# A gated linear-attention kernel: gates with two steps per partition, un-permuted in 64-row matmuls, with sine and cosine from two PSUM banks

## The chip, the cores and the metric

The kernel runs on one core of one Trainium2 chip. The metric is the device time of that core in microseconds (us), as a median over several executions. Engines are named as in the profile: PE is TensorE, PEld its weight loads, DVE is VectorE, ACT is ScalarE, POOL is GpSimd, SP issues DMAs. The profile also shows PEclk, the share of its full clock that TensorE was granted.

A run is called slow when its time is over 1.5% above the fastest run of the same kernel.

## The reference, cut to what matters

Two parts follow each other. The first is a linear attention with a complex decay, for 4 batches, 8 heads, 768 steps and a head width of 48. The second is a layer norm with a two-layer MLP of widths 384, 1536 and 384.

```python
mag = np.sqrt(a_re*a_re + a_im*a_im)
scale = np.minimum(mag, 0.999) / (mag + 1e-06)
a_re_n, a_im_n = a_re*scale, a_im*scale
for t in range(S):
    new_re = ar*S_re - ai*S_im          # ar, ai: step t of a_re_n, a_im_n, per row of the state
    new_im = ar*S_im + ai*S_re
    S_re, S_im = new_re + k[t] (x) v[t], new_im
    y[t] = q[t] @ S_re
# x = y with the heads side by side: (4, 768, 384)
xn = (x - mean) / sqrt(var + 1e-06) * g_ln
out = x + relu(xn @ w_ch1) @ w_ch2
```

Over a chunk of 128 steps, the product of the decays is the exponential of a running sum of logarithms (`l`), and its angle is a running sum of angles (`th`). So the kernel computes running sums by triangular matmuls, takes `exp`, `sin` and `cos`, multiplies them into q and k, and then works with plain matmuls per chunk: scores `at`, output `y`, state `G`. There are 24 chunks.

## The kernel before

The gates are made for a group of three chunks at a time. A step of the sequence is a partition. The calls are put in order by a plan with real-number positions, and each engine runs its own list in that order.

The gates and the running sum of the logarithms:

```python
def g_decay(g, cs):                       # DVE
    nc.vector.scalar_tensor_tensor(out=cut(l, cs), in0=cut(G[g]["u"], cs), scalar=0.5,
                                   in1=cut(G[g]["w"], cs), op0=ALU.mult, op1=ALU.add)
    nc.vector.tensor_scalar(out=cut(l, cs), in0=cut(l, cs), scalar1=LNCAP,
                            scalar2=LNEPS, op0=ALU.min, op1=ALU.add)

def s_decay(g, c):                        # one 128-row matmul, two exponentials
    nc.tensor.matmul(ps, lhsT=u_f, rhs=row(G[g]["l"], c), start=True, stop=True)
    special(out=row(e, c), in_=ps, func=AF.Exp)
    special(out=row(en, c), in_=ps, func=AF.Exp, scale=-1.0)
```

The phase: PE adds the angles and the phase carried in from the last chunk (`car`). DVE adds a constant that puts the fraction of a turn in the low 16 bits. POOL reads the last row back as the next carry. Sine comes from ACT, and cosine from DVE by a half-angle formula:

```python
def s_phase(g, c, eng=nc.gpsimd):
    nc.tensor.matmul(ps, lhsT=u_th, rhs=row(G[g]["th"], c), start=True, stop=first)
    if not first:
        nc.tensor.matmul(ps, lhsT=last[96:C, :], rhs=X[n - 1]["car"][96:C, :],
                         start=False, stop=True)
    nc.vector.tensor_scalar(out=row(ph, c), in0=ps, scalar1=WINDOW, scalar2=None, op0=ALU.add)
    if n % NCH < NCH - 1:
        eng.tensor_scalar(out=X[n]["car"][96:C, :], in0=turns(row(ph, c)[96:C]),
                          scalar1=1.0 / TURN, scalar2=None, op0=ALU.mult)

def s_cos(g, cs):
    nc.vector.tensor_tensor(out=cut(hq, cs), in0=cut(hs, cs), in1=cut(hs, cs), op=ALU.mult)
    nc.vector.tensor_scalar(out=cut(cos, cs), in0=cut(hq, cs), scalar1=-2.0, scalar2=1.0,
                            op0=ALU.mult, op1=ALU.add)
```

The MLP weights are scaled by `g_ln` once, on DVE, and centred into a second copy. The first MLP layer has one PSUM buffer `hps`:

```python
def scale(dc):
    nc.vector.tensor_scalar(out=W["w1b"][:, dc], in0=W["w1b"][:, dc],
                            scalar1=W["gln"][:, ds(dc, 1)], scalar2=None, op0=ALU.mult)

def mm1(jp):
    ps = ph.tile([C, 2, 512], FP32, tag="h", name="hps")     # pool ph: bufs=1
    ...                                                       # cut: six matmuls into ps
    nc.scalar.activation(out=st["h"][:, ts(jp, 2)], in_=ps[:, :, 0:GC * C], func=AF.Relu)
```

## Time and profile before

The time was 280.08 us, the median of three runs (278.67 to 282.95; the last is just over 1.5% above the first and so counts as slow).

The first view is the page: busy times with the share of the span and the instruction count, then the span in 40 slices of 7 us (a digit is the busy share in tenths; PEclk is the granted clock in tenths), then the chain of work that ended last, by engine ("issue" is time in which an engine waited for nothing that the profile shows).

```profile
PE 207.4 (74%) x1915; PEld 136.4 (49%) x1917; DVE 197.2 (71%) x328; ACT 175.4 (63%) x247; POOL 99.3 (36%) x107
...
PE   0321542747849996989799969988998999998673
DVE  0679906999699669986997699689848946633001
PEclk9999999999786998999799979997999999999999
...
PE 33%; DVE 32%; ACT 12%; issue 11%; POOL 8%; DMA 2%; POOLq 0%; DVEq 0%; ACTq 0%
```

No engine is full over the whole span, and the chain of waits divides itself equally between PE and DVE. The slices show why an average misleads here: DVE is at 9 in places from slice 4 on and fades at the end, while PE reaches 9 only in slice 13 (84 us).

The second view is the window view of the same trace. Its columns are the stretch in us, its length, the busy time (and instruction count) of PE, PEld, DVE, ACT and POOL, then PEclk, the DMA share and GB/s.

```profile
0.00:60.00 60.00, 21.26 (x132) 12.91 (x132) 39.03 (x61) 37.49 (x53) 26.18 (x42) 1.00 1.31 176
60.00:100.00 40.00, 30.51 (x274) 19.96 (x277) 34.63 (x62) 24.48 (x35) 18.00 (x16) 0.87 1.23 184
100.00:245.00 145.00, 132.12 (x1363) 90.60 (x1362) 117.23 (x194) 104.67 (x147) 55.08 (x50) 0.95 0.34 66
245.00:279.00 34.00, 23.47 (x151) 12.91 (x148) 6.36 (x14) 8.76 (x14) 0.00 (x0) 1.00 0.10 35
```

Before 60 us PE has little to do. In the long middle PE is busy for 132 of 145 us and DVE for 117.

The third view is the groups of instructions, by form: line, engine, operation, tiles, shape and count, then busy us and mean ns, then idle us before it.

```profile
L230 DVE SCALAR_TENSOR_TENSOR l<-u,w 128x1152 f16<-128x1152 f16 x7 | 27.2, 3886 | 3.0 <-ACT u L196 3.0
...
L281 POOL TENSOR_SCALAR car<-ph 32x384 f16<-32x384 int16 x17 | 22.1, 1300 | 79.6 <-DVE ph L277 78.5 <-ACT en L196 0.8
...
L159 DVE TENSOR_SCALAR w1b<-w1b,gln 128x1536 bf16<-128x1536 bf16 x3 | 1.9, 617 | 0.0
```

The step `l` takes 3.89 us for 1152 elements, though with POOL not in its way it takes 0.5 to 0.55 us for 384 (three such calls at the start).

Two timelines of the same moment, DVE and then POOL, show why `l` is slow. The columns are start, duration, and the instruction.

```profile
130.36 4.08 DVE L230 SCALAR_TENSOR_TENSOR l<-u,w 128x1152 f16<-128x1152 f16 x1 [0.39 <-ACT u L196]
```

```profile
130.58 2.64 POOL L301 TENSOR_TENSOR qe<-q,e 128x384 bf16<-128x384 f32 x3
```

While POOL works through its three products, `l` makes no progress to speak of: `l` ends 1.2 us after the last product, and 4.08 us less 2.64 us is 1.44 us, near its free time. The Trainium skill ("SBUF — State Buffer", section "Who interferes with whom") says that DVE and GpSimd share a port pair under an exclusive lock. This trace agrees.

One timeline of PE shows a phase before the change: one full-height matmul, one 32-row carry, and then the next work.

```profile
90.02 0.33 PE L273 MATMUL tps<-th,u_th 128*128 128x384 f16 x1
90.27 0.33 PE L275 MATMUL tps<-car,last 32*128 32x384 f16 x1
90.54 0.50 PE L416 MATMUL o<-w2b,h 128*128 128x384 bf16 x2
```

The durations overlap (0.33 us at starts 0.25 us apart), so starts are what to read: from 90.02 to 90.54 is 0.52 us for a phase. The starts after a change of row height are 0.25 to 0.27 us apart, while equal 384-column matmuls follow each other every 0.162 us (six in 1.14 us, the last one ending about 0.33 us after its start).

The last timeline is the tail, PE and ACT together.

```profile
258.85 1.14 PE L407 MATMUL hps<-xT,w1c 128*128 128x384 bf16 x6 [0.90 <-ACT h L410]
...
260.02 0.81 ACT L410 ACTIVATE h<-hps 128x768 bf16<-128x768 f32 x1 [1.22 <-PE hps L407]
...
260.88 1.14 PE L407 MATMUL hps<-xT,w1c 128*128 128x384 bf16 x6 [0.57 <-ACT h L410]
```

With one `hps` buffer the matmuls and their eviction (ACT's copy out of PSUM) take turns.

### The profile page before, as it was taken

The numbers are of one execution on the slowest core, as the hardware profiler recorded it, in microseconds if no ns is written. First come the engines' busy times: TensorE is split into PE (matmuls) and PEld (weight loads), VectorE is DVE, ScalarE is ACT, GpSimd is POOL, SyncE is SP. The second block draws the span as 40 slices with busy tenths as digits, with TensorE's granted clock in tenths as the row PEclk, the third lists the DMA queues.
The fourth block names the chain that finished last, engine by engine and source line by source line (L and its number), as shares of the span: only waits on it lengthen the run. The fifth ranks groups of instructions, "written<-read, shape, count | busy, mean of one in ns | idle before, by whom it ended". The sixth has DMA issues, their size and how long they took to land.

```text
span 279.1 us, 4840 instructions
## 1 busy us (share of the span) xinstructions
PE 207.4 (74%) x1915; PEld 136.4 (49%) x1917; DVE 197.2 (71%) x328; ACT 175.4 (63%) x247; POOL 99.3 (36%) x107
## 2 busy tenths in 40 slices
PE   0321542747849996989799969988998999998673
PEld 0000221734536664757475737564656667764331
DVE  0679906999699669986997699689848946633001
ACT  6682483754695588688777858884679663541420
POOL 4069106703870275057706530763148100000000
PEclk9999999999786998999799979997999999999999
DMA  7999999999999966473790370000000101001001
GB/s 155 214 219 184 136 196 184 142 161 190 217 194 160 159 150 134 94 151 73 152 138 2 73 153 31 2 28 31 28 2 28 60 0 59 28 2 56 28 31 56
DMA packets 130310, 28.62 MB, mean 103 GB/s; under 512 B 125296, under 2 KB 129904, under 8 KB 130288
## 3 DMA queue, kind: packets, MB, share of 16 engines
q1 hardware_dynamic: 103696, 23.60, 43.6%
q0 software_dynamic: 26592, 4.72, 20.5%
q8 instruction: 15, 0.25, 0.3%
q14 instruction: 7, 0.06, 0.1%
HBM read 28.31 MB, written 4.72 MB: 118 GB/s over the span
## 4 chain that ended last, share of the span: by engine, by line
PE 33%; DVE 32%; ACT 12%; issue 11%; POOL 8%; DMA 2%; POOLq 0%; DVEq 0%; ACTq 0%
PE o L416 14%; PE hps L407 10%; DVE l L230 7%; POOL car L281 6%; ACT h L410 4%; DVE atm L334 3%; DVE ot L421 3%; DVE ks L307 2%; DVE l L232 2%; DVE stats L371 2%; DVE qs L307 2%; ACT u L196 2%; DVE ph L277 2%; DVE hq L295 1%; PE tot L254 1%
## 5 line engine op out<-in xcount | busy, mean ns | idle before, releaser
L410 ACT ACTIVATE h<-hps 128x768 bf16<-128x768 f32 x48 | 38.8, 809 | 49.4 <-PE hps L407 49.1
L416 PE MATMUL o<-w2b,h 128*128 128x384 bf16 x288 | 62.6, 353 | 5.7 <-DVE ot L421 4.6
L407 PE MATMUL hps<-xT,w1c 128*128 128x384 bf16 x288 | 55.9, 330 | 4.7 <-ACT h L410 3.8
L281 POOL TENSOR_SCALAR car<-ph 32x384 f16<-32x384 int16 x17 | 22.1, 1300 | 79.6 <-DVE ph L277 78.5
L416 PEld LDWEIGHTS <-h 128*128 128x128 bf16 x288 | 28.6, 104 | 25.7 <-issue 11.8
L407 PEld LDWEIGHTS <-w1c 128*128 128x128 bf16 x288 | 27.8, 99 | 23.6 <-issue 9.6
L334 DVE TENSOR_TENSOR atm<-at,mask 128x512 bf16<-128x512 f32 x48 | 32.5, 679 | 3.7 <-PE at L332 3.7
L421 DVE SCALAR_TENSOR_TENSOR ot<-o,rstd,x 128x384 f32<-128x384 f32 x24 | 14.7, 611 | 26.2 <-PE o L416 25.8
L230 DVE SCALAR_TENSOR_TENSOR l<-u,w 128x1152 f16<-128x1152 f16 (+1 forms) x10 | 28.8, 2886 | 3.0 <-ACT u L196 3.0
L322 ACT COPY qsT<-tp 96x1024 bf16<-96x1024 bf16 x24 | 24.1, 1004 | 7.8 <-PE tp L320 7.8
L192 ACT ACT_TABLE_LOAD x19 | 24.4, 1283 | 1.1 <-PEq L526 0.7
L332 PE MATMUL at<-qsT,ksT 96*128 96x128 bf16 x192 | 21.0, 230 | 3.2 <-DVE G L353 2.3
L220 DVE TENSOR_TENSOR r<-aim,rinv 128x1152 f16<-128x1152 f32 (+1 forms) x10 | 11.1, 1111 | 16.9 <-DMA aim<-in_a_im_dram 10.1
L301 POOL TENSOR_TENSOR ke<-k,en 128x384 bf16<-128x384 f32 x24 | 21.6, 908 | 0.8
L307 POOL TENSOR_TENSOR qs<-qe,sin 128x1152 bf16<-128x1152 bf16 x7 | 16.9, 2418 | 11.9 <-ACT sin L196 11.9
L301 POOL TENSOR_TENSOR qe<-q,e 128x384 bf16<-128x384 f32 x24 | 21.2, 903 | 0.0
L320 PE MATMUL tp<-ident,ks 128*96 128x128 bf16 x192 | 18.6, 244 | 2.6 <-DVE ks L307 1.7
L332 PEld LDWEIGHTS <-ksT 96*128 96x128 bf16 x192 | 15.2, 104 | 10.4 <-issue 7.9
L320 PEld LDWEIGHTS <-ks 128*96 128x96 bf16 x192 | 16.1, 142 | 8.2 <-issue 4.7
L322 DVE COPY ksT<-tp 96x1024 bf16<-96x1024 bf16 x24 | 16.3, 681 | 4.4 <-PE tp L320 4.3
L320 PE MATMUL tp<-ident,qs 128*96 128x128 bf16 x192 | 18.7, 238 | 0.2 <-ACT x L369 0.2
L320 PEld LDWEIGHTS <-qs 128*96 128x96 bf16 x192 | 16.1, 137 | 5.6 <-issue 3.5
(88 smaller groups left out, 379.1 us busy)
## 6 DMA issues: line engine op xcount, KB each, us to landing
are<-in_a_re_dram SPq DMA_DIRECT2D x24, 192.0 KB, 3.8
aim<-in_a_im_dram SPq DMA_DIRECT2D x24, 192.0 KB, 3.8
k<-in_k_dram SPq DMA_DIRECT2D x24, 192.0 KB, 3.8
q<-in_q_dram SPq DMA_DIRECT2D x24, 192.0 KB, 3.9
out_dram<-ot SPq DMA_DIRECT2D x24, 192.0 KB, 1.9
v<-in_v_dram POOLq DMA_DIRECT2D x4, 576.0 KB, 15.5
w1b<-in_moe_w_ch_dram POOLq DMA_DIRECT2D x1, 1152.0 KB, 19.0
w2b<-in_moe_w_ch_dram POOLq DMA_DIRECT2D x1, 1152.0 KB, 26.3
```

The source lines that it names most:

```text
L192: chain(nc.scalar.preload_act_table_set({"log": "natural_log_exp_and_others", "trig": "trig_and_small"}[name]))
L230: nc.vector.scalar_tensor_tensor(out=cut(l, cs), in0=cut(G[g]["u"], cs), scalar=0.5, in1=cut(G[g]["w"], cs), op0=ALU.mult, op1=ALU.add)
L281: eng.tensor_scalar(out=X[n]["car"][96:C, :], in0=turns(row(ph, c)[96:C]), scalar1=1.0 / TURN, scalar2=None, op0=ALU.mult)
L301: nc.gpsimd.tensor_tensor(out=row(t, c), in0=row(G[g][which], c), in1=row(G[g]["en" if which == "k" else "e"], c), op=ALU.mult)
L307: eng.tensor_tensor(out=t[:, cs, :, a].rearrange("p c h d -> p (c h) d"), in0=heads(G[g][which + "e"]), in1=heads(G[g]["sin" if a else "co ...
L320: nc.tensor.transpose(ps[:, h], st[which][:, c, h].rearrange("p a d -> p (a d)"), ident)
L322: (nc.scalar.copy if which == "qs" else nc.vector.tensor_copy)(out=t, in_=ps)
L332: nc.tensor.matmul(ps[:, i], lhsT=x["ks"][:, h], rhs=x["qs"][:, h], start=True, stop=True)
L334: nc.vector.tensor_tensor(out=x["atm"][:, ds(half * (H // 2), H // 2)], in0=ps, in1=mask.unsqueeze(1).to_broadcast([C, H // 2, C]), op=ALU ...
L407: nc.tensor.matmul(ps[:, ji, 0:GC * C], lhsT=W["w1c"][:, dc, ts(j, C)], rhs=st["xT"][:, dc].rearrange("p c t -> p (c t)"), start=(dc == 0) ...
L410: nc.scalar.activation(out=st["h"][:, ts(jp, 2)], in_=ps[:, :, 0:GC * C], func=AF.Relu)
L416: nc.tensor.matmul(st["o"], lhsT=st["h"][:, j, ts(c, C)], rhs=W["w2b"][:, j], start=(j == 0), stop=(j == NJ - 1))
```

## The change

The intent is to take work off DVE, POOL and ACT, and to give some of it to PE. (In the code below, "stacks" are the products of the scaled q or k with sine and cosine, `lps` holds the running sums of logarithms, `tot` their totals per chunk, `tps` the phases, and `dps` the totals laid out for the state.) A group is now four chunks. A partition holds two consecutive steps, so `a_re` and `a_im` arrive in runs of 384 bytes. Chunks come out of this layout in the matmuls: the steps of one chunk lie in 64 partitions, so each running sum is made of two 64-row matmuls. Cosine is the sine of the phase plus a quarter turn: the phase is computed twice, into two PSUM banks, and one ACT call takes both. The carry comes in by a 128-row matmul with a selecting matrix `pick`, whose right-hand side also holds the constants. DVE takes the next carry from PSUM.

The core of the diff, cut (`...`) and joined to one line here and there:

```diff
-    GC = 3
+    R = 2                        # steps per partition
+    QC = 4                       # chunks per group
-    pa = ... bufs=5              # PSUM banks
-    ph = ... bufs=1              # two banks, hps
-    po = ... bufs=1              # o
+    pa = ... bufs=4
+    pb = ... bufs=2              # two banks each: lps, tps, at, hps in turn
...
 # weights
-            nc.vector.tensor_scalar(out=W["w1b"][:, dc], in0=W["w1b"][:, dc],
-                                    scalar1=W["gln"][:, ds(dc, 1)], ...)
+        nc.gpsimd.tensor_scalar(out=w1b[:, dc], in0=w1b[:, dc], scalar1=gln[:, ds(dc, 1)], ...)
...
 # running sum of logarithms, two chunks at a time
-        nc.tensor.matmul(ps, lhsT=u_f, rhs=row(G[g]["l"], c), start=True, stop=True)
+        for j in range(R):
+            for i in range(R):
+                nc.tensor.matmul(heads(ps[:, i]), lhsT=u_f[ts(i, HALF), j],
+                                 rhs=steps(Q[qi]["l"], k_, i, j), start=(j == 0),
+                                 stop=(j == R - 1))
...
 # phase of one chunk
-        nc.tensor.matmul(ps, lhsT=u_th, rhs=row(G[g]["th"], c), ...)
-        nc.tensor.matmul(ps, lhsT=last[96:C, :], rhs=X[n - 1]["car"][96:C, :], ...)
-        nc.vector.tensor_scalar(out=row(ph, c), in0=ps, scalar1=WINDOW, ...)
-        eng.tensor_scalar(out=X[n]["car"][96:C, :], in0=turns(row(ph, c)[96:C]), ...)
+        for s in range(2):                        # sine bank, cosine bank
+            for j in range(R):
+                nc.tensor.matmul(heads(ps[:, s]), lhsT=u_th[ts(i, HALF), j],
+                                 rhs=steps(Q[qi]["th"], k_, i, j), start=(j == 0), stop=False)
+            nc.tensor.matmul(ps[:, s, 0:DM], lhsT=pick[rows, s], rhs=cars[n % 2][rows],
+                             start=False, stop=True)
+        nc.vector.tensor_scalar(out=cars[(n + 1) % 2][96:C], in0=v16[96:C, 0],
+                                scalar1=1.0 / TURN, ...)
+        special(out=trig[:, m], in_=v16, func=AF.Sin, scale=TWO_PI_SAFE / TURN)
-    s_cos: hq = hs * hs; cos = 1 - 2 hq           # DVE, both gone
...
 # stacks: one of four was on POOL, now all on DVE; scores evicted in one piece of 1024
 # plan: new table of positions (PLACES), new order of the start
```

## The prediction

> **What bounds the kernel now.** No engine is saturated: the page gives PE 74%, DVE 71%, ACT 63%, POOL 36% of 279.1 us. By stretches of the window view: 0-45 us is startup (first transposes at 32.6 us; DVE then waits 7.8 us for `aim`, behind crowded DMA); 45-165 us has DVE busy 103 of 120 us and PE 96; 165-254 us is PE (82 of 89 us); from 254 us there is a tail of 25 us, of which 12 us is `hps` matmuls and the `h` eviction taking turns (1.15 + 0.82 us, one buffer). The chain of waits says the same: PE 33%, DVE 32%, ACT 12%, issue 11%, POOL 8% (almost all `car`).
>
> **Removed.** DVE: `ph` 13.2 us, `hq` 6.3, `cos` 3.9, `w1b` scaling 1.9. POOL: `car` 22.1 and one `qs` stack 16.9 (about 39 of 99 us). ACT: about 4.5 us of exponentials (two chunks per instruction), 2 of `h`, 3 of gates, about five table loads of 1.28 us. DVE `atm` in one piece saves about 3.5.
>
> **Port sharing.** `l` takes 3.9 us for 1152 elements while `qe` runs on POOL and 0.55 us for 384 without; so 41 us of the two `l` steps should be near 14 unblocked. The Trainium skill ("SBUF - State Buffer", Who interferes with whom) says that a DVE instruction with two SBUF inputs blocks against a GpSimd instruction that reads SBUF; this trace agrees: `l` ends as the last `qe` ends. `ke`/`qe` stay on POOL, so I count on half of these 27 us only.
>
> **Added.** DVE: `car` read from PSUM, about 20 x 0.5 = 10 us, and stacks +6 us (48 of about 0.54). PE: a phase is six 384-column matmuls per chunk in place of two, a decay sum four per two chunks instead of two: 124 more matmuls. Warm spacing is 0.162 us (six `hps` in 1.14 us), so about 20 us, plus about 0.09 us at each change between 64 and 128 rows (the 32-row `car` matmul shows such a gap: next start 0.25-0.27 us later). The skill ("TensorEngine Tiling (Array Packing)", Key Properties) says that changing the mode drains the array. Together about 25 us of PE occupancy, estimated.
>
> **Sum.** From spacings I estimate real PE occupancy of 177 us now, about 200 after; DVE falls from 197 to about 175-185; ACT about 170; POOL about 60-65. So PE becomes the limit in the middle, but it has slack there. Gains on the critical path: startup works on two chunks first and `a` arrives in 384-byte pieces, so first transposes at about 20 us (-10); the wait on `aim` (-5); no POOL step in the phase chain, less blocking of DVE in the middle (-12); two `hps` buffers in the tail (-5 net, though the last group has four chunks). Against: PE work in the middle (+8).
>
> **Prediction: 257 us**, 8 in 10 between 240 and 275. Faster by over 2%: 0.84; within 2%: 0.10; slower by over 2%: 0.06.
>
> **What would show it.** First transposes near 20 us; POOL busy near 65 us; DVE below 190 us, `l` at 1.8-3 us per 1536 elements; PE busy above 225 us; tail after the last `xT` under 20 us with `hps` back to back; PE as the largest part of the chain.
>
> **What would make it wrong.** The two double-bank PSUM buffers now carry decay sums, phases, score blocks and `hps` in turn: if ACT is late with a sine, PE stalls in order, and the serial phase chain (PE, DVE `car`, PE) shows up as waits of PE. If mode changes cost more than 0.1 us, PE adds over 40 us and the gain vanishes. If the stacks, now all on DVE, collide with `ke`/`qe`, DVE gets no shorter.

## More of the kernel before

From 60 to 100 us DVE is the busiest engine (34.6 of 40).

The weight scaling is a small item: three times 0.62 us.

## The result, and the profile after

The change gave 270.19 us, the median of four runs (269.37 to 270.54), beside 280.93 us for the kernel before in the same rounds. The ratio is 0.964, with a 95% interval of 0.957 to 0.971. A ratio here and below is the mean time of a kernel's fast runs over that of the other's fast runs of the same rounds, so it is not quite the ratio of the quoted medians.

So the kernel became faster by 3.6%. The forecast was 257 us, which is 8.2%. So less than half of the expected gain came.

The page after, the same parts as before and the POOL slices as well (a slice is 6.7 us now):

```profile
PE 212.0 (79%) x1953; PEld 124.1 (46%) x1953; DVE 173.9 (65%) x277; ACT 171.8 (64%) x199; POOL 80.2 (30%) x93
...
PE   0146733389302999999999999999999999999994
...
DVE  1334238658999789985799656987578466645011
...
POOL 8390009442996770009400091000910000000000
PEclk9999999999955699999999999999999999999999
...
PE 60%; ACT 19%; DVE 15%; POOL 3%; issue 2%; POOLq 0%; DVEq 0%; ACTq 0%
```

Two things stand out. From slice 14 on, PE is at 9 in all slices but the last. Before that, in slices 11 to 13 (67 to 87 us), PE falls to 3, 0 and 2, and its granted clock to 5, 5 and 6 right after. In these slices POOL is at 9, 9 and 6.

The window view after:

```profile
0.00:60.00 60.00, 25.48 (x170) 11.76 (x170) 26.78 (x37) 30.97 (x35) 26.20 (x47) 1.00 1.05 189
60.00:100.00 40.00, 23.42 (x214) 12.20 (x213) 35.35 (x41) 26.57 (x29) 29.32 (x18) 0.79 1.28 173
100.00:245.00 145.00, 143.55 (x1463) 89.60 (x1463) 106.84 (x191) 107.12 (x130) 24.66 (x28) 1.00 0.33 62
245.00:268.00 23.00, 19.59 (x111) 10.49 (x109) 4.92 (x10) 7.12 (x9) 0.00 (x0) 1.00 0.16 61
```

In the middle PE is busy for 143.6 of 145 us: it has become a stream without gaps. From 60 to 100 us PE did less than before (23.4 us and 214 instructions, against 30.5 and 274), and POOL did more (29.3 against 18.0).

To see what each stage gained, follow one milestone: the moment at which ACT evicts the attention output `x` of a chunk. Here is the fourth one, first from the timeline of ACT before, then after.

```profile
85.05 0.48 ACT L369 CAST x<-y 128x384 bf16<-128x384 f32 x1 [0.31 <-PE y L366]
```

```profile
96.38 0.48 ACT L496 CAST x<-y 128x384 bf16<-128x384 f32 x1 [0.80 <-PE y L493]
```

| stretch | before, us | after, us | difference |
|---|---|---|---|
| start to the 4th output | 85.1 | 96.4 | +11.3 |
| 4th to the last output (20 chunks) | 166.2 | 148.6 | -17.6 |
| last output to the end | 27.9 | 23.4 | -4.5 |
| span | 279.1 | 268.4 | -10.7 |

The first output comes at 55.6 us, where it was at 54.5. The second comes at 59.6 us (before, 65.4), and only then does the new kernel fall behind: the third comes at 78.9 us (before, 76.0). The border between the first two rows is not sharp: at its fourth output the new kernel has evicted the decays of 12 chunks, the old one those of 9. In the MLP it is not ahead: its first MLP eviction starts at 105.3 us, before at 87.7 us. So the 11.3 us are no exact measure of a loss; the experiments measure that.

Three timelines of the hole after the change, DVE, POOL and PE:

```profile
71.96 3.34 DVE L334 TENSOR_TENSOR r_616<-r 128x1536 f16<-128x1536 f16 x1
...
76.95 4.19 DVE L346 SCALAR_TENSOR_TENSOR l<-r_616,w 128x1536 f16<-128x1536 f16 x1
81.17 4.40 DVE L348 TENSOR_SCALAR l<-l 128x1536 f16<-128x1536 f16 x1
```

```profile
69.69 5.67 POOL L278 TENSOR_SCALAR w1b<-w1b,gln 128x1536 bf16<-128x1536 bf16 x1
...
76.25 8.91 POOL L278 TENSOR_SCALAR w1b<-w1b,gln 128x1536 bf16<-128x1536 bf16 x2
```

```profile
70.41 0.61 PE L452 MATMUL at<-qsT,ksT 96*128 96x128 bf16 x8
85.63 1.44 PE L381 MATMUL tot<-l,sel 128*4 128x384 f16 x4 [14.61 <-DVE l L348]
```

The weight scaling, moved to POOL, runs from 69.7 to 75.4 us and from 76.3 to 85.2 us. The DVE steps end about when POOL's end: the square at 75.3 us, the second `l` at 85.6 us. The next matmul of PE's list needs `l`, so PE stands still from 71 to 85.6 us. The groups view after gives the size of the moved step:

```profile
L278 POOL TENSOR_SCALAR w1b<-w1b,gln 128x1536 bf16<-128x1536 bf16 x3 | 14.6, 4863 | 0.0
```

It is 14.6 us where it was 1.9 us.

The waits of PE after the change (what it waited for, us in total, times, longest):

```profile
PE lps L368 <- DVE l L348: 20.7, 3, 11.2
PE tot L381 <- DVE l L348: 14.6, 1, 14.6
```

Both lines are waits for `l`: of the running sums (`lps`) and of the totals (`tot`). The three of the first line end at 11.2, 35.0 and 51.5 us, in the start.

PE's timeline for one phase after, answering to the three lines of before (the matmuls marked `tp` are other work put between):

```profile
126.35 0.50 PE L406 MATMUL tps<-th,u_th 64*128 64x384 f16 x2
...
127.14 0.33 PE L409 MATMUL tps<-car_124,pick 128*128 128x384 f16 x1
127.40 0.50 PE L406 MATMUL tps<-th,u_th 64*128 64x384 f16 x2
127.83 0.34 PE L409 MATMUL tps<-car_124,pick 128*128 128x384 f16 x1
```

From 127.14 to 127.83 us is 0.69 us for one bank of three matmuls, so a chunk's phase takes 1.38 us of PE, against 0.52 us. Of that, each change between 64 and 128 rows costs about 0.1 us (a start gap of 0.26 or 0.27 us, instead of 0.162 us).

The tail after, from PE's timeline:

```profile
248.86 7.93 PE L524 MATMUL hps<-xT,w1b 128*128 128x512 bf16 x36
256.63 7.96 PE L534 MATMUL o<-w2b,h 128*128 128x384 bf16 x48
```

Two `hps` buffers removed the turns: 36 matmuls back to back, then 48.

### The profile page after: what moved, and what is told of

Same layout as the page of the kernel before. It is cut to its first block, busy times and chain, and to the rows that moved or that the text cites. A ratio compares the mean times of both kernels' runs of the same rounds, so it can differ in the third digit from the quotient of the medians.

```text
span 268.4 us, 4759 instructions
## 1 busy us (share of the span) xinstructions
PE 212.0 (79%) x1953; PEld 124.1 (46%) x1953; DVE 173.9 (65%) x277; ACT 171.8 (64%) x199; POOL 80.2 (30%) x93
## 2 busy tenths in 40 slices
DMA packets 105350, 28.62 MB, mean 107 GB/s; under 512 B 100336, under 2 KB 104944, under 8 KB 105328
## 4 chain that ended last, share of the span: by engine, by line
PE 60%; ACT 19%; DVE 15%; POOL 3%; issue 2%; POOLq 0%; DVEq 0%; ACTq 0%
PE o L534 16%; PE hps L524 11%; PE tps L406 8%; PE tp L440 6%; PE tps L409 5%; PE at L452 3%; DVE l L346 3%; PE lps L368 2%; ACT h L527 2%; ACT are L309 2%; ACT L305 2%; ACT w L309 2%; DVE r L332 2%; DVE l L348 2%; PE gm L474 2%
## 5 line engine op out<-in xcount | busy, mean ns | idle before, releaser
L524 PE MATMUL hps<-xT,w1b 128*128 128x512 bf16 x216 | 51.7, 378 | 0.2 <-ACT h L527 0.2
L534 PE MATMUL o<-w2b,h 128*128 128x384 bf16 x288 | 50.8, 326 | 0.0
L527 ACT ACTIVATE h<-hps 128x1024 bf16<-128x1024 f32 x36 | 36.5, 1021 | 11.6 <-PE hps L524 11.4
L309 ACT ACTIVATE trig<-tps 128x768 bf16<-128x768 int16 x24 | 19.5, 811 | 26.9 <-DVE car_124 L413 16.9
L534 PEld LDWEIGHTS <-h 128*128 128x128 bf16 x288 | 27.1, 98 | 17.6 <-issue 1.6
L454 DVE TENSOR_TENSOR atm<-at,mask 128x1024 bf16<-128x1024 f32 x24 | 29.2, 1217 | 7.5 <-PE at L452 7.3
L406 PE MATMUL tps<-th,u_th 64*128 64x384 f16 x96 | 26.3, 357 | 8.2 <-ACT th L309 8.2
L524 PEld LDWEIGHTS <-w1b 128*128 128x128 bf16 x216 | 19.6, 98 | 18.9 <-issue 0.5
L368 PE MATMUL lps<-l,u_f 64*128 64x384 f16 x48 | 7.7, 420 | 20.7 <-DVE l L348 20.7
L496 ACT CAST x<-y 128x384 bf16<-128x384 f32 x24 | 11.3, 472 | 13.5 <-PE y L493 13.5
L332 DVE TENSOR_TENSOR r<-aim,are 128x1536 f16<-128x1536 f32 (+1 forms) x7 | 11.7, 1665 | 11.8 <-ACT are L309 11.8
L381 PE MATMUL tot<-l,sel 128*4 128x384 f16 x24 | 6.9, 417 | 14.6 <-DVE l L348 14.6
L498 DVE BATCH_NORM_STATS2 stats<-x 128x6 f32<-128x384 bf16 x24 | 13.3, 554 | 6.8 <-ACT x L496 6.7
## 6 DMA issues: line engine op xcount, KB each, us to landing
w1b<-in_moe_w_ch_dram POOLq DMA_DIRECT2D x1, 1152.0 KB, 11.3
```

Of the source, the lines that this page charges most:

```text
L309: chain(nc.scalar.activation(**kw))
L332: nc.vector.tensor_tensor(out=cut(r, bs), in0=cut(Q[qi]["aim"], bs), in1=cut(Q[qi]["are"], bs), op=ALU.mult)
L406: nc.tensor.matmul(heads(ps[:, s]), lhsT=u_th[ts(i, HALF), j], rhs=steps(Q[qi]["th"], k_, i, j), start=(j == 0), stop=False)
L454: nc.vector.tensor_tensor(out=x["atm"], in0=ps, in1=mask.unsqueeze(1).to_broadcast([C, H, C]), op=ALU.mult)
L524: nc.tensor.matmul(ps[:, ji], lhsT=w1b[:, dc, ts(jp * 2 + ji, C)], rhs=Q[qi]["xT"][:, dc].rearrange("p c t -> p (c t)"), start=(dc == 0), ...
L527: nc.scalar.activation(out=h[jp], in_=ps, func=AF.Relu)
```

## The experiments

Two theories came from the traces. The first says that the moved weight scaling is the lost gain: it takes POOL eight times as long, it holds the port that DVE needs, and PE starves behind DVE and then runs at half clock. The second, its rival, says that PE's added work is the lost gain: PE has no gap in the middle, so each added microsecond is paid in full. Two more came up later: that ACT's table loads between the logarithm and sine sets make the early hole, and (called theory L) that the order of the first logarithms sets the start. Eighteen kernels were run; all gave the right result unless it is said.

A gain over the change that is given below in us is the difference of the two ratios to before, times the time of the change. The intervals of the ratios make such a difference uncertain by 2 to 3 us. The milestones of the section before help where this is too coarse: each is read from one trace.

### 1. The weight scaling back on DVE, at the same place

```diff
-        nc.gpsimd.tensor_scalar(out=w1b[:, dc], in0=w1b[:, dc], ...
+        nc.vector.tensor_scalar(out=w1b[:, dc], in0=w1b[:, dc], ...
```

> The changed kernel with the three weight scalings (1536 elements each) back on DVE; the order on PE, ACT and SP is the same. Theory S (starved start): on POOL they took 14.6 us, blocked the decay steps of DVE, and PE stood still from 71 to 85.6 us; since PE is a gap-free stream afterwards, what is lost early is never won back. Then the gap is gone and the time falls by 8 to 14 us, to 256 to 262 us. Rival R (PE has enough other waits early, so the gap only moves): 266 us or more.

It took 269.91 us (267.12 to 271.25), ratio 0.956 (0.950 to 0.963), not clear of the change. Theory S's figure was missed; the rival's held. Its profiled run was a slow one (clock 0.918), so only the order of events is read from it. The timeline of DVE says what happened:

```profile
57.34 3.15 DVE L278 TENSOR_SCALAR w1b<-w1b,gln 128x1536 bf16<-128x1536 bf16 x3 [5.73 <-DMA w1b<-in_moe_w_ch_dram]
```

In DVE's list the scaling now stands ahead of the scores of the first chunks, and the weights have not landed yet. DVE waited 5.73 us for them, and PE behind it. The hole moved rather than closed. This run does not test the first theory; runs 5 and 6 do.

### 2. The two carries of a phase after its four 64-row matmuls

```diff
         for s in range(2):
             for j in range(R):
                 nc.tensor.matmul(heads(ps[:, s]), lhsT=u_th[ts(i, HALF), j], ...)
+        for s in range(2):
             nc.tensor.matmul(ps[:, s, 0:DM], lhsT=pick[rows, s], ...)
```

> The changed kernel with each chunk's four 64-row phase matmuls first and its two 128-row carry matmuls after them: two changes of rows per chunk in place of four; same matmuls. Theory P (PE is the limit after 85 us and each change of rows costs about 0.1 us): a phase takes about 1.18 us of PE instead of 1.38, 16 chunks lie after 85 us, so 3 to 4 us less, 266 to 267 us. Rival (PE's stream has slack, or the changes of rows cost nothing): 269.5 us or more.

It took 266.87 us (265.90 to 268.51), ratio 0.950 (0.945 to 0.954), as expected. A phase now has two changes of row height and not four. From the start of its four 64-row matmuls to the start of the next chunk's is 1.19 us in PE's timeline, with the two carries in between, against 1.38 us:

```profile
124.14 0.82 PE L405 MATMUL tps<-th,u_th 64*128 64x384 f16 x4
...
125.33 0.82 PE L405 MATMUL tps<-th,u_th 64*128 64x384 f16 x4
```

That is 0.19 us times 24 chunks, or 4.6 us, and the time fell by 1.5% (0.9639 to 0.9495), about 4 us. This fits what the start gaps say of the changes of row height, with an uncertainty of over 2 us. By the milestones, 1.0 us came before the fourth output and 2.1 us between it and the last. The Trainium skill ("TensorEngine Tiling (Array Packing)", section "Key Properties") says that a change of tiling mode drains the engine; the run agrees, and gives the size.

### 3. No cosine bank (wrong result)

```diff
-        for s in range(2):                 # the matmuls of a phase
+        for s in range(1):
...
-        special(out=trig[:, m], in_=v16, ...)
+        special(out=trig[:, m], in_=v16[bank 0].to_broadcast([C, 2, DM]), ...)
```

> The changed kernel with the cosine bank's three matmuls of each phase left out and both planes of sines read from the first bank: a wrong result on purpose. Theory P: 0.69 us of PE per chunk goes, 16 chunks lie after 85 us, so about 11 us less, 257 to 261 us. Rival (the added matmuls hide in PE's waits): 267 us or more.

It took 262.24 us (261.70 to 263.14), ratio 0.933 (0.930 to 0.936). The relative error is 0.60, as intended. Leaving out three matmuls per chunk takes 24 x 0.69 = 16.6 us of PE away, and the time fell by 3.2%, about 8.8 us. So about half of that work was on the path to the end. Not all of it can be: in the first 90 us PE waits for others. The fourth output comes only 0.5 us earlier than in the change (95.8 us), and the stretch from it to the last falls from 148.6 to 141.3 us.

### 4. The kernel before, with the weight scaling on POOL

```diff
-            nc.vector.tensor_scalar(out=W["w1b"][:, dc], ...
+            nc.gpsimd.tensor_scalar(out=W["w1b"][:, dc], ...
```

> The kernel before, with only its three weight scalings moved from DVE to POOL. Theory S says that this move alone costs time when it meets DVE's decay steps: 4 to 12 us more than before. Rival R: within 2 us of before, or less, since DVE is relieved by 1.9 us.

It took 285.09 us (284.37 to 286.98), ratio 1.015 (1.010 to 1.020). This one line makes the old kernel about 4 us slower. (The interval is clear of 1.) Its groups view shows the same slow step: three instructions on POOL, 14.6 us together, 4.88 us each.

### 5. No weight scaling at all (wrong result)

```diff
-        nc.gpsimd.tensor_scalar(out=w1b[:, dc], in0=w1b[:, dc], scalar1=gln[:, ds(dc, 1)],
-                                scalar2=None, op0=ALU.mult)
```

> The changed kernel with the three weight scalings left out (a wrong result on purpose); the order on every engine is otherwise the same. Putting them on DVE only moved the hole in PE's stream, because DVE then waited 5.7 us for the weights to land. Theory S: without them on POOL, r, l and their followers on DVE lose about 9 us of blocked time between 68.9 and 85.6 us, the hole closes by that much, and nothing later gives it back: 260 to 264 us. Rival T (the hole is set by ACT, which loads its tables four times there): 267 us or more.

It took 263.55 us (262.64 to 263.77), ratio 0.939 (0.934 to 0.943), with a relative error of 0.47. The order of all other instructions is unchanged. That is 2.6% less than the change, about 7 us. DVE's timeline, at the place of the hole:

```profile
72.13 0.95 DVE L334 TENSOR_TENSOR r<-r 128x1536 f16<-128x1536 f16 x1
...
76.82 1.76 DVE L346 SCALAR_TENSOR_TENSOR l<-r,w 128x1536 f16<-128x1536 f16 x1 [2.15 <-ACT r L309]
78.61 0.56 DVE L348 TENSOR_SCALAR l<-l 128x1536 f16<-128x1536 f16 x1
```

The three steps take 0.95, 1.76 and 0.56 us. With POOL busy beside them they took 3.34, 4.19 and 4.40 us. PE's wait for `tot` fell from 14.6 to 6.5 us. The two windows from 75 to 90 us, the change first and then this run:

```profile
75.00:90.00 15.00, 4.37 (x17) 0.99 (x18) 13.63 (x13) 7.35 (x9) 11.32 (x6) 0.50 0.99 222
```

```profile
75.00:90.00 15.00, 10.55 (x73) 4.88 (x75) 10.70 (x18) 12.18 (x15) 7.55 (x8) 0.66 1.03 227
```

PE does 73 instructions here and not 17. The granted clock is 0.50 in the first and 0.66 in the second. The Trainium skill ("TensorE: Matmul & The Clock Gate", section "What's actually happening") says that the clock is halved after an idle window; both windows agree with that. The lowered clock is not what differs. In narrower windows it stays at 0.50 for about 6 us after PE starts again, in both: from 85.6 to 91.8 us in the change and from 79.2 to about 85.3 us here. What differs is the standstill: PE starts again 6.4 us earlier. And the lead stays. The fourth output comes 6.4 us earlier than in the change (96.38 us),

```profile
89.94 0.48 ACT L496 CAST x<-y 128x384 bf16<-128x384 f32 x1 [0.80 <-PE y L493]
```

the stretch from it to the last output is 148.6 us in both kernels, and the span is 6.4 us shorter (262.0 us).

### 6. The weight scaling on DVE, after the second chunk's statistics

```diff
-        nc.gpsimd.tensor_scalar(out=w1b[:, dc], ...
+        ins = nc.vector.tensor_scalar(out=w1b[:, dc], ...
+        # order only: not before the statistics (bn_aggr) of chunk 1, on the same engine
```

> The changed kernel with the weight scalings on DVE and held back, by an ordering edge, until the statistics of chunk 1 are done, so that the weights have landed. Theory S: as with no scaling, less the 2 us of DVE work: 262 to 266 us. Rival T: 267 us or more.

It took 262.84 us (262.11 to 264.02), ratio 0.937 (0.932 to 0.942). A correct kernel has the gain that run 5 showed, 2.8% or about 7 us. The fourth output comes at 90.3 us, and the stretch to the last is 148.6 us again. So the first theory holds for 7 us, except for its half clock, and it was the place in DVE's list, not the engine, that spoilt run 1.

### 7. Fewer table loads on ACT, the scaling still on POOL

```diff
 PLACES group 1: 'phase_step': 0.59 -> 0.28
 PLACES group 2: 'angle': -0.31 -> 1.06,  'table_log': -1.2 -> -0.9
```

> The changed kernel with four places moved so that the sines of group 1 all come ahead of the logarithms of group 2 on ACT: the six table loads that ACT had to put in between are gone (7.7 us of ACT). Weight scaling stays on POOL. Theory T: the decay chain of group 2 runs about 5 us earlier and PE's hole closes by that much: 262 to 266 us. Theory S says that DVE is blocked by POOL whatever ACT does: 268 us or more.

It took 280.49 us (276.27 to 280.98); its two fast runs (276.27 and 280.27 us) give a ratio of 0.992 (0.981 to 1.002). Theory T's figure was missed; theory S's, 268 us or more, held. Four of the 21 table loads of 1.28 us were gone, where six were expected, but now the stacks came to stand beside POOL's scaling. From DVE's timeline (a slow run):

```profile
81.20 4.03 DVE L428 TENSOR_TENSOR ks<-ke,trig 128x768 bf16<-128x768 bf16 x2
```

Such a pair takes 1.00 us in run 5. This is one more case of the blocked port, and no test of the table loads.

### 8. The phases of two chunks side by side

The 64-row matmuls of two chunks are issued in turn, one on rows 0 to 63 and one on rows 64 to 127, into two two-bank buffers. Then the carries follow.

```diff
-        ps = two_banks("tps")
-        ...                                # per bank: two 64-row matmuls, one carry
+        if i == 0:
+            X[n]["tps"], X[n + 1]["tps"] = two_banks("tps"), two_banks("tps")
+            for s, j, a in [(s, j, a) for s in range(2) for j in range(R) for a in range(R)]:
+                nc.tensor.matmul(heads(X[n + a]["tps"][:, s]), lhsT=u_th[ts(a, HALF), j],
+                                 rhs=steps(Q[qi]["th"], k_, a, j), start=(j == 0), stop=False)
```

> The changed kernel with the 64-row phase matmuls of two chunks issued in turn on rows 0 to 63 and 64 to 127, as the decay sums are (their four took 0.43 us, not 0.65), and the carries after them. Theory P: about 1.2 us of PE less for each pair of chunks, eight pairs lie after 85 us: 9 to 10 us less, 260 to 262 us. Rival Q (two double banks held from the pair's start to the second chunk's sine keep decay sums, scores and the first MLP product waiting): 268 us or more.

It took 260.51 us (259.60 to 262.56), ratio 0.929 (0.923 to 0.935), as expected: 3.6% less than the change, about 9.7 us. PE's timeline:

```profile
118.89 0.82 PE L406 MATMUL tps<-th,u_th 64*128 64x384 f16 x8
119.64 0.50 PE L411 MATMUL tps<-car,pick 96*128 96x384 f16 x2
```

Eight matmuls take 0.75 us from start to start. In run 2, four of one half took as long. So the two halves of the array work at the same time, as the skill's tiling page says in the same section. With two pairs of carries at 0.44 us each (in run 2, 1.19 less 0.75 us), two chunks take an estimated 1.63 us, against 2.76 us in the change: 13.6 us over 24 chunks.

The 9.7 us are not simply the part of this that reached the end. In the trace the span is 10.5 us shorter, and 6.3 us of that come before the fourth output (90.1 us), where PE's wait for `tot` fell from 14.6 to 8.8 us. Only 4.3 us come between the fourth output and the last. Why the new order shortens the early wait was not tested.

### 9. Runs 6 and 8 together

> Both repairs of the changed kernel: weight scalings on DVE after chunk 1's statistics, and phase matmuls in pairs. If the hole in the start and the phase matmuls of the full part are two separate losses (theories S and P), the gains of 2.7 and 3.5 per cent add: a ratio to before of 0.90 to 0.91, 252 to 256 us. If they are one loss counted twice: 0.925 or more, 259 us or more.

The edit is the two diffs above. It took 255.63 us (254.68 to 256.71), ratio 0.914 (0.906 to 0.923), as expected. The single gains were 2.8% and 3.6% of the time of the change; together they give 5.1%, less than the sum, though within its uncertainty. By the milestones the pairs still give 4.3 us after the fourth output, but 4.1 us before it and not 6.3. In the rounds of runs 9 to 12, four of the seven runs of the kernel before were slow, and the record calls the verdict against it unclear; these four runs are best compared with each other.

### 10. Run 9 with the positions of run 7

> The same with the sines of group 1 ahead of the logarithms of group 2. With scaling on POOL that reordering cost time, since four products of DVE, now ahead of the decay steps, were blocked by POOL for 3 to 4 us a pair. If that was the cause, the reordering without scaling on POOL costs nothing and saves up to 3 us against both repairs: 249 to 256 us. If the reordering itself is bad: 262 us or more.

It took 259.24 us (258.83 to 260.87), ratio 0.928 (0.921 to 0.936), which is worse than run 9 in the same rounds. Both figures of the expectation were missed. PE's wait for `tot` is 9.2 us, against 4.9 us in run 9. Why the new positions make this wait long was not followed up, so the part that table loads play stays open.

### 11. Run 9, with the MLP weights fetched and scaled later

```diff
-    seq += [lambda: load_w()]
+    add(2.2, load_w)
 PLACES: 'w_lo': 2.93 -> 4.55, 'w_hi': 6.07 -> 6.37     # and the order of run 6 by chunk 2
```

> Both repairs, and the MLP weights (2.3 MB) fetched only after the first products with k of group 1. POOL waited 7 us for k while the weights were arriving. If that crowding set the second hole of PE (66 to 69 us in the changed kernel), the time falls by 1 to 4 us against both repairs, to 249 to 254 us; if k was not on the path, within 1 us of both repairs; if the weights now land too late for the first MLP product, more than both repairs.

It took 254.43 us (253.94 to 254.62), ratio 0.910 (0.904 to 0.915). In the same rounds its four runs all lie below the four of run 9, by 1.2 us in the median. That is at the low edge of what was expected, and too small to say more.

### 12. Run 9, with two small constants made first on POOL

```diff
+    one_b = ...; eps_b = ...     # two memsets, now ahead of POOL's other constants
     ident = consts.tile([C, C], BF16)
```

> Both repairs, and the two bias constants made first on POOL instead of last: ACT waited 2.9 us for them in the first logarithm, of which about 1.2 us was after its data were ready. If the serial start (decay, angle, phase of the first two chunks) is on the path to the end, about 1 us less than both repairs: 251 to 255 us; if the start is slack, the same.

It took 258.76 us (257.51 to 260.09), ratio 0.926 (0.918 to 0.933): slower than run 9, and a miss. The build also put other instructions in another order, so the run says nothing about the constants alone.

### 13. The first group's logarithms and decays ahead of the first sine

```diff
-           lambda: g_log(0, one(1)), lambda: g_ratio(0, one(1)), lambda: table("trig"),
+           lambda: g_log(0, one(1)), lambda: g_ratio(0, one(1)), lambda: g_log1p(0, one(1)),
+           lambda: g_decay(0, one(1)), lambda: s_decay(0, 1), lambda: s_total(0),
+           lambda: table("trig"),
```

> The changed kernel, but both blocks of group 0 go through their logarithms and decays before the first sine, as in the kernel before; all else as it was. Theory L (the split start loses its lead because the second block's decays wait behind the first block's sines): the first attention output comes 3 to 5 us earlier than 55.6 us. The hole of PE from 71 us is bound by POOL's weight scaling, which is not moved, so the total falls by 0 to 3 us: 267 to 271 us. Rival: the first output is later, since the first sine is, and the total rises.

It took 268.06 us (267.80 to 268.58), ratio 0.958 (0.951 to 0.964). The first output came at 54.5 us, where 3 to 5 us less than the 55.6 us of the change were expected. Theory L is not supported.

### 14. Runs 11 and 13 together

> Both repairs, the late weight fetch, and the start as in logs_first. Here nothing on POOL blocks group 2's decays, so a gain in the start should reach the end: theory L 250 to 252 us (a ratio to before 1 to 1.7 per cent lower than without). Rival (the start is not on the path): 254 us or more.

It took 253.45 us (252.23 to 253.93), ratio 0.905 (0.898 to 0.911). First output at 53.4 us. The time lies between the two expectations and decides nothing.

### 15 and 16. The second copy of the chunk totals by ACT, not POOL

```diff
-        nc.gpsimd.tensor_copy(out=et[:, :, 1], in_=et[:, :, 0])
+        special(out=et[:, :, 1], in_=ps.rearrange("p (h d) -> p h d", d=D), func=AF.Exp)
```

On top of run 14:

> The same, and both copies of the chunk totals made by ACT from PSUM (0.46 us each) in place of a copy on POOL. If PE's in-order wait on the POOL copy is what is left of the start's loss: 1 to 2 us less again, 248 to 251 us. If not: within 1 us.

On top of run 11:

> Both repairs, the late weight fetch and the totals on ACT, with the changed kernel's order of the start. If the POOL copy alone loses the lead: 1.5 to 3 us less than 254.4 us. If the order of the start is the cause (theory L): within 1 us of it.

They took 255.48 us (254.93 to 256.79), ratio 0.913 (0.905 to 0.921), a miss, and 253.65 us (253.19 to 254.21), ratio 0.906 (0.900 to 0.913), within 1 us as in the second case. The copy of 0.73 us on POOL, which PE waits for (`dps`, 4.9 us in the change), is not what holds these kernels up.

### 17. The change, with group 1's running sums after the first output

```diff
 PLACES group 1: 'sum': 0.72 -> 1.06, 'total': 0.75 -> 1.10
```

> The changed kernel with group 1's decay sums and totals placed behind the output of chunk 0 (two places moved). Theory O (PE's in-order wait at those sums swallows the start's lead): the first output comes at 45 to 48 us in place of 55.6. The sums themselves still wait for DVE, and the hole from 71 us is bound by POOL, so the total falls by at most 3 us: 266 to 271 us. Rival: the first output stays at 53 to 56 us.

In all these kernels PE stands at the running sums of group 1, in the change from 45.1 to 51.5 us, while the first chunk's scores could already be used, because PE runs its list in order. This edit puts that wait behind the first output (in total it is 20.2 us, before the edit 20.7): the output came at 49.1 us, 6.4 us earlier. But the next came at 59.6, 80.6 and 97.1 us, against 59.6, 78.9 and 96.4 us in the change, and the time was 271.05 us (270.73 to 271.74), ratio 0.965 (0.960 to 0.970), the same as the change within the intervals. So this lead of the first output did not reach the end.

### 18. Run 14 with the edit of run 17

> Both repairs, the late weight fetch, the decays of group 0 first and group 1's sums behind the output of chunk 0. Theory O: the first output at 45 to 48 us. If the start is on the path to the end, 1 to 3 us less than 253.5 us, a ratio of 0.895 to 0.90; if the path runs through DVE's decay steps of groups 1 and 2 whatever PE does meanwhile, within 1 us of it.

It took 253.00 us (252.65 to 253.42), ratio 0.900 (0.895 to 0.905). Of the correct kernels this is the fastest median; its interval overlaps that of run 14. The first output came at 42.3 us, 11 us earlier than in run 14, and the time stayed within 1 us, as in the last case of the expectation. It beats both given kernels: about 10% below before, and by the ratios 0.900 and 0.964 about 6.6% below the change. In its page POOL is busy for 64.5 us, where the prediction had put it for the change, and DVE for 165.1 us.

| kernel | median, us | ratio to before | 95% interval |
|---|---|---|---|
| the change | 270.19 | 0.964 | 0.957 to 0.971 |
| 1 scaling on DVE, same place | 269.91 | 0.956 | 0.950 to 0.963 |
| 2 carries last | 266.87 | 0.950 | 0.945 to 0.954 |
| 3 no cosine bank (wrong) | 262.24 | 0.933 | 0.930 to 0.936 |
| 4 before, scaling on POOL | 285.09 | 1.015 | 1.010 to 1.020 |
| 5 no scaling (wrong) | 263.55 | 0.939 | 0.934 to 0.943 |
| 6 scaling on DVE, later | 262.84 | 0.937 | 0.932 to 0.942 |
| 8 phases in pairs | 260.51 | 0.929 | 0.923 to 0.935 |
| 9 runs 6 and 8 | 255.63 | 0.914 | 0.906 to 0.923 |
| 18 best | 253.00 | 0.900 | 0.895 to 0.905 |

## Why the prediction was wrong

The direction was right and the size was not: 257 us were forecast, 270.19 us came. The sum in the prediction was -15 us in the startup, -12 + 8 = -4 us in the middle, and -5 us in the tail.

**The startup term failed.** The prediction said of it: "so first transposes at about 20 us (-10); the wait on `aim` (-5)". The first transposes came at 27.5 us (before, at 32.6 us), and the fourth output came 11.3 us later than before, not 15 us earlier. The waits of DVE for `aim` (10.1 us) did go, but the same step `r` now waits 11.8 us for ACT where it waited 6.7 us. Three findings stand in its place.

1. The part that is shown is the weight scaling. The prediction counted it as 1.9 us taken off DVE, and never asked what it would take on POOL. It took 14.6 us there, and it stretched three DVE steps from 3.3 us (run 5) to 11.9 us (the change). Runs 5 and 6 show its cost: 7 us by the ratios, 6.4 us in the trace of run 5. Run 4 shows 4 us of cost in the kernel before. The prediction had described this very blocking, and had used it only in favour of the change: it counted what POOL no longer does, and not the new work that POOL was given in the start.
2. The 5 us lead of the first transposes is lost before the first output. PE runs in order, and stands at group 1's running sums. Run 17 puts that stand behind the first output, and the time stays the same. So even that lead of the first output was worth nothing.
3. Without the scaling the fourth output still comes at 89.9 us (run 5), 4.9 us later than before. So some 20 us between this and the -15 us of the forecast have another cause, and it stays open what holds outputs 3 and 4 in place. ACT's table loads and late k and q are candidates; runs 7 and 10 were meant to test the first of these and changed too much else.

**The added PE work was sized about rightly; that its share on the path was too low is not clear.** The prediction said "Against: PE work in the middle (+8)", out of an estimated 25 us. The trace gives 1.38 - 0.52 = 0.86 us more per phase, or 21 us for 24 chunks, and 0.1 us at each change of row height, as estimated. The slack that the prediction counted on ("it has slack there") is used up: PE was busy for 132 of 145 us before, and for 143.6 us after. Run 3 measures the share most cleanly: 8.8 of 16.6 us reached the end, so 21 us cost an estimated 11 us and not 8. Run 2 has a higher share, 4 of 4.6 us, with an uncertainty of over 2 us. The 9.7 us of run 8 are no such measure, since most of them came before the fourth output. About 14 of the 24 phases lie after that output. There the three runs took away an estimated 9.7, 2.7 and 7.9 us of PE, and the stretch to the last output fell by 7.3, 2.1 and 4.3 us. At these shares, a half to nearly eight tenths, the added work of that stretch (12 of the 21 us) costs an estimated 6.5 to 9.5 us, near the 8 us that were forecast.

**The middle gained more than forecast.** From the 4th to the last output the time fell by 17.6 us, where -4 us net were forecast. Here the argument held better than its own numbers: `ph`, `hq`, `cos` and POOL's `car` are gone, the unblocked `l` takes 1.76 us, and DVE's part of the chain fell from 32% to 15%. How the gain divides between these was not tested. Part of it may belong to the startup, since the border at the fourth output is not sharp.

**The tail was right**: -4.5 us against -5, and 36 `hps` matmuls back to back.

**The signs that the prediction named.** DVE below 190 us: right, 173.9. `l` at 1.8 to 3 us: right when unblocked, 1.76, though 4.19 and 4.40 us in the hole. PE as the largest part of the chain: right, 60%. First transposes near 20 us: wrong, 27.5. POOL near 65 us: wrong, 80.2, and the 14.6 us of scaling are the whole excess. The five table loads that were to go: wrong, there are 21 after (14 of them called for by the plan, 7 put in where a function needed the other set) and 19 before. PE busy above 225 us: wrong, 212.0, since the busy time of the two MLP layers fell between the two traces, from 118.5 us (55.9 + 62.6) to 102.5 us (51.7 + 50.8) in the groups view, which the prediction had not counted. Of its warnings, a serial phase chain on PE hardly shows (0.2 us of waits for `car`); the row-height changes stayed at 0.1 us; the stacks on DVE did not collide with `ke` and `qe` on average (0.55 and 0.57 us each).

Together: of the 13 us between forecast and result, about 7 us are the weight scaling (shown), and about 3 us are an estimate for PE's added work beyond the 8 us counted, no larger than its uncertainty. By the milestones the startup missed its term by 26 us, of which the scaling is 6.4, and the middle beat its term by 14 us. The runs do not say what the other 20 us of the startup are, nor how much of these two misses is one quantity counted on both sides of the border. The forecast came as near as it did because they have opposite signs, which is luck.

## What to carry to other kernels

Cost an operation that moves on the engine that it moves to, with that engine's own duration, and then ask which instructions of other engines stand beside it and what they share: here, three instructions of 0.62 us became 4.86 us each, blocked DVE, and kept PE standing 6.4 us longer. When an engine has become a stream without gaps, a half or more of a change in its work reached the end here, and a standstill earlier was not won back (148.6 us from the fourth to the last output, with and without it), while a lead of a single early result was worth nothing. When matmuls of different heights alternate, group them by height, and issue the two halves of the rows in turn: that gave 9.7 us here without changing what is computed, though only 4.3 us of it in the stretch where PE is full.

## What the Trainium skill lacked or had wrong

- "GPSIMD Engine Reference", section "4.1 Engine selection", advises against GpSimd for elementwise work, but calls work with one input roughly line-rate there. Here a multiplication of 128 x 1536 bf16 by a per-partition scalar took 4.86 and 4.88 us on POOL (means of three, in two kernels, in part beside steps of DVE that it blocked) and 0.62 us on DVE, nearly eight times less. The 32 x 384 carry took 1.30 us on POOL.
- "TensorEngine Tiling (Array Packing)", section "Key Properties", says that a mode change drains the engine, and gives no cost. Between 64-row and 128-row matmuls of 384 columns the start gap was 0.26 to 0.27 us instead of 0.162 us, so about 0.1 us each. Halving the number of changes saved about 4 us, uncertain by 2 us.
